# Attention and a squared-ReLU feed-forward on one core: the seven half-size products in another order, their joins on GpSimd, and queued work spread out

## The chip, the cores and the metric

The kernel runs on one core of a Trainium2 chip. A core has five engines that work through queues of their own: TensorE (PE; its weight loads are listed apart as PEld), VectorE (DVE), ScalarE (ACT), GpSimd (POOL) and SyncE (SP), which here issues the DMAs. They wait for each other by semaphores. SBUF is the on-chip memory of 128 partitions, PSUM the eight banks into which TensorE writes. The metric is the device time of one execution in microseconds (us). Every number is float32, and one float32 matmul of the program appears in the trace as two records ("passes").

## The reference

Eight batches of twelve heads, 448 rows, head dimension 64. Rows of q and k are normalized, softmax attention follows, the heads are put side by side (3584 tokens x 768), and a feed-forward layer with squared ReLU ends it:

```python
q_n, k_n = (rmsnorm(q, g_q), rmsnorm(k, g_k))
attn = softmax(q_n @ k_n.T / sqrt(64))      # per batch and head
x = (attn @ v).transpose(0, 2, 1, 3).reshape(3584, 768)
h = np.maximum(x @ w_in, 0.0)               # w_in 768 x 2048
out = (h * h) @ w_out                       # w_out 2048 x 768
```

w_in and w_out arrive as 64-bit numbers and are turned into float32 on the chip ("words").

## The kernel before, in words

**Feed-forward.** It runs in four passes u = 0 to 3, each over two batches (896 rows), and each pass in NBLK = 4 blocks of hidden columns. A block has a first product (x by w_in), the activation, and a second product (hidden by w_out, added into nine accumulators, `accs`). Both products are done with seven half-size products instead of eight (Strassen-Winograd, `PRODUCTS`: for instance P5 = S1 x T1), for which sums of operands are made beforehand: of w_in (S1 to S4), of w_out (T1 to T4), of x (`form_steps`) and of the hidden values (`hidden_sum`, L1037, on GpSimd: s1 = a21 + a22, s2 = s1 - a11, s4 = a12 - s2, s3 = a11 - a21).

In pass 0, `first_products` (L870) does the first product at this one level, while the weights are still converted (`convert`: load of words, three ScalarE instructions L1198 to L1200, three VectorE instructions L1211, L1231, L1235), the sums made (`make_sum`, L1304) and the sums for a second level are written to DRAM (`deep_steps`, L1271 and L1272, pieces `in_deep`). In passes 1 to 3, `deep_products` does each of the seven products at the second level again (11 matmuls of 224 columns, L921, in steps `step(k, 0..3)`), with pieces loaded four products ahead (`load_piece`, L798). `DEEP` lists the seven in order, with the place of each result: four quarters of the hidden tiles "11", "12", "21", "22", or a room "R". `put` moves a result out of PSUM: a copy on ScalarE where there is no base, else an addition on VectorE (L908). Where "R" holds a partial sum, more L908 additions join it to "12", "22" and "21". `activate` does Relu and Square on ScalarE (L977, L978); the last half of "21" is done by one VectorE instruction (L1014).

`second_products` (L1095) then runs, for each of three row tiles tt, the products in `SECOND_ORDER`, with `multiply_rest` (L1050) for the remaining 128 rows; `add_to` (L1138, VectorE) adds PSUM to the accumulator, or copies on ScalarE in block 0 (L1136). Three PSUM banks (`roles`) rotate; bank 1 also serves as `aside` in the deep products, banks 0 to 4 belong to attention.

**Attention.** It runs over 48 pairs of heads. The first batches are done before the feed-forward starts; afterwards a visit to a pair (`visit_among`, `visit_whole`) is put between steps of the feed-forward: scores (L405), exponentials on ScalarE (`weigh`, L413), values (L490), denominators (L533, L542), sums of weights on GpSimd (`add_up`, L432). `place(u, x)` says at which cost a visit comes. `ffn(u)` is a generator whose steps yield a cost (`COST_IN`, `COST_OUT`, `COST_DEEP`); `run(until)` takes steps until that cost is spent, and after each step lets queued work go: one weight sum, the end of a conversion, conversions that are due (`late`), up to two steps of the next pass's forms (`follow_plan(2)`), and one or two each of `tasks` and `pool_tasks` (`run_tasks`). A visit first runs all that is left of both queues. The instructions of each engine run in the order in which this program issues them.

**Transfers.** All loads and stores go through SyncE's queue in order: q and k rows (L157, L166), v (L348, L355), q rows to DRAM and back in blocks (`store_q` L314 and L320, `load_blocks` L330), words (L1179, L1184), half-size weights (L798), w_out's forms (L803), results (L1143). A DMA that waits for its source or its room holds back those behind it.

## Time and profile before

| | |
|---|---|
| median of 6 runs | 1460.32 us (1456.67 to 1463.01) |
| the profiled execution | 1462.95 us |
| its span, first to last instruction | 1460.8 us |
| mean granted TensorE clock | 0.988 |
| DMAs | 229.04 MB, q1 53.7% of 16 engines |

A group of the profile reads: line, engine, operation, out<-in by names, shapes, count | busy time, mean ns of one | idle time of the engine before them and what ended it. "bank L533 <- ACT wT L413: 14.4, 3, 5.5" in the list of waits means that TensorE's matmuls of line 533 waited for the ScalarE instruction of line 413 for 14.4 us in all, three times, at most 5.5. A row of busy time by stage gives a stretch, its length, busy time and number of instructions per engine, the granted clock (1.00 is full speed) and DMA.

### The profile page before, as it was taken

The numbers are of one execution on the slowest core, as the hardware profiler recorded it, in microseconds if no ns is written. First come the engines' busy times: TensorE is split into PE (matmuls) and PEld (weight loads), VectorE is DVE, ScalarE is ACT, GpSimd is POOL, SyncE is SP. The second block draws the span as 40 slices with busy tenths as digits, with TensorE's granted clock in tenths as the row PEclk, the third lists the DMA queues.
The fourth block names the chain that finished last, engine by engine and source line by source line (L and its number), as shares of the span: only waits on it lengthen the run. The fifth ranks groups of instructions, "written<-read, shape, count | busy, mean of one in ns | idle before, by whom it ended". The sixth has DMA issues, their size and how long they took to land.

```text
span 1460.8 us, 18011 instructions
## 1 busy us (share of the span) xinstructions
PE 1397.4 (96%) x5772; PEld 840.7 (58%) x5772; DVE 849.6 (58%) x1727; ACT 563.7 (39%) x1078; POOL 745.9 (51%) x750
## 2 busy tenths in 40 slices
PE   7989999899898989999999989999999999999998
PEld 3333444344443466665857548575676658678694
DVE  5996566687677754355544755345464665254554
ACT  6874466445555233341432323433332302221120
POOL 5667764656556865365473863736463462020201
PEclk9999999999999999999999999999999999999999
DMA  5555746767748874562747547265554426233232
GB/s 143 148 159 154 194 123 160 217 169 201 233 113 262 241 211 140 142 179 73 228 106 230 138 138 222 69 190 137 173 136 144 145 72 234 95 118 144 69 141 78
DMA packets 362219, 229.04 MB, mean 157 GB/s; under 512 B 270084, under 2 KB 339588, under 8 KB 358020
## 3 DMA queue, kind: packets, MB, share of 16 engines
q1 hardware_dynamic: 361824, 227.74, 53.7%
q8 instruction: 47, 0.77, 0.2%
q14 instruction: 56, 0.46, 0.1%
q10 hardware_dynamic: 292, 0.07, 0.0%
HBM read 172.49 MB, written 55.25 MB: 156 GB/s over the span
## 4 chain that ended last, share of the span: by engine, by line
PE 79%; DVE 6%; DMA 4%; issue 3%; POOL 3%; SPq 2%; ACT 2%; DVEq 0%; POOLq 0%; ACTq 0%
PE bank L1095 28%; PE bank L921 21%; PE bank L405 8%; PE bank L490 8%; PE bank L870 6%; PE bank L1050 5%; DVE hid L908 2%; DMA words<-in_moe_w_out_dram 1%; DMA in_sb<-in_deep 1%; PE bank L516 1%; SPq L157 1%; PE bank L533 1%; PE bank L502 1%; ACT wT L413 1%; POOL sum L432 1%
## 5 line engine op out<-in xcount | busy, mean ns | idle before, releaser
L921 PE MATMUL bank<-xT,in_sb 128*128 128x224 f32 x1344 | 294.7, 358 | 10.2 <-DMA in_sb<-in_deep 5.4
L1138 DVE TENSOR_TENSOR acc<-acc,bank 128x384 f32<-128x384 f32 x324 | 173.2, 549 | 215.5 <-PE bank L1095 188.8
L1095 PE MATMUL bank<-out_sb,hid 128*128 128x384 f32 x768 | 268.8, 487 | 3.8 <-DVE acc L1138 3.8
L921 PEld LDWEIGHTS bank<-xT,in_sb 128*128 128x128 f32 x1344 | 255.5, 192 | 24.4 <-issue 8.7
L1095 PE MATMUL bank<-out_sb,sums 128*128 128x384 f32 x576 | 204.5, 490 | 5.2 <-DVE acc L1138 5.2
L1095 PEld LDWEIGHTS bank<-out_sb,hid 128*128 128x128 f32 x768 | 145.2, 190 | 108.7 <-DVE acc L1138 6.6
L413 ACT ACTIVATE wT<-bank,rr 128x448 f32<-128x448 f32 x288 | 161.5, 630 | 114.3 <-PE bank L405 95.0
L202 POOL TENSOR_TENSOR rr<-ms,minus_half 128x8 f32<-128x8 f32 (+1 forms) x96 | 146.9, 1530 | 63.1 <-DVE ms L195 57.5
L1037 POOL TENSOR_TENSOR sums<-hid 128x384 f32<-128x384 f32 x32 | 32.9, 1028 | 274.8 <-ACT hid L978 238.1
L405 PE MATMUL bank<-qT,kT 64*128 64x448 f32 (+1 forms) x768 | 166.6, 576 | 2.1 <-DVE qT L378 1.1
L1095 PEld LDWEIGHTS bank<-out_sb,sums 128*128 128x128 f32 x576 | 107.4, 190 | 90.9 <-DVE acc L1138 10.7
L870 PE MATMUL bank<-xT,in_sb 128*128 128x448 f32 x336 | 137.1, 563 | 0.0
L908 DVE TENSOR_TENSOR part<-part,bank 128x224 f32<-128x224 f32 (+1 forms) x180 | 69.7, 415 | 97.8 <-PE bank L921 92.0
L405 PEld LDWEIGHTS bank<-qT,kT 64*128 64x128 f32 (+1 forms) x768 | 57.6, 174 | 99.6 <-issue 67.4
L432 POOL TENSOR_TENSOR sum<-sum,wT 128x448 f32<-128x448 f32 (+1 forms) x96 | 113.4, 1199 | 0.8
L870 PEld LDWEIGHTS bank<-xT,in_sb 128*128 128x128 f32 x336 | 64.6, 197 | 72.6 <-issue 65.0
L490 PE MATMUL bank<-wT,vt 128*64 128x448 f32 x480 | 102.8, 549 | 0.0
L977 ACT ACTIVATE hid<-hid 128x448 f32<-128x448 f32 x84 | 48.4, 576 | 130.2 <-DVE hid L908 130.2
L1050 PE MATMUL bank<-out_sb,hid 128*128 128x384 f32 x256 | 90.4, 491 | 0.0
L554 POOL COPY few<-few 32x14 f32<-32x14 f32 x48 | 9.0, 188 | 155.1 <-DVE few L552 153.1
L908 DVE TENSOR_TENSOR hid<-hid,bank 128x224 f32<-128x224 f32 (+1 forms) x180 | 66.6, 397 | 31.0 <-PE bank L921 28.6
L921 PE MATMUL bank<-more,in_sb 128*128 128x224 f32 x288 | 75.1, 362 | 6.9 <-DVE part L908 6.0
(131 smaller groups left out, 1871.2 us busy)
## 6 DMA issues: line engine op xcount, KB each, us to landing
in_sb<-in_deep SPq DMA_DIRECT2D x84, 640.0 KB, 4.2
out_sb<-out_forms SPq DMA_DIRECT2D x24, 1536.0 KB, 8.6
words<-in_moe_w_in_dram SPq DMA_DIRECT2D x32, 384.0 KB, 3.7
words<-in_moe_w_out_dram SPq DMA_DIRECT2D x32, 384.0 KB, 3.4
out_forms<-out_sb SPq DMA_DIRECT2D x8, 1536.0 KB, 6.4
qk<-in_q_dram SPq DMA_DIRECT2D x96, 96.0 KB, 3.0
qk<-in_k_dram SPq DMA_DIRECT2D x96, 96.0 KB, 2.6
vt<-in_v_dram SPq DMA_DIRECT2D x96, 96.0 KB, 3.1
```

The costliest lines, as they stand in the source:

```text
L202: self.nc.gpsimd.tensor_tensor(out=self.rr[i][:, x, 0 : self.count(i)], in0=ms, in1=self.minus_half.to_broadcast(list(ms.shape)), op=ALU.pow,)
L405: nc.tensor.matmul(sc[some], lhsT=turned[p, 1][r, keys], rhs=turned[p, 0][r, :], start=True, stop=True,)
L413: nc.scalar.activation(new_weights((i, m), e), sc, AF.Exp, scale=rows.rr[i][:, 1, 2 * m + e : 2 * m + e + 1],)
L432: nc.gpsimd.tensor_tensor(out=sums[i, e][some], in0=left[some], in1=weights[key_of(i, m), e][some], op=ALU.add)
L490: nc.tensor.matmul(values_bank(i)[ds(e * D, D), :], lhsT=lasts[i % 2][mine, e, :] if m == NJ else values[i][:, m, e, :], rhs=weights[key_o ...
L870: nc.tensor.matmul(ps, lhsT=w_sb[:, IN.index(left), c, :], rhs=forms[u, c][right], start=first and c == 0, stop=c == NK - 1, skip_group_ch ...
L908: nc.vector.tensor_tensor(out=dst, in0=left, in1=right, op=ALU.add)
L921: nc.tensor.matmul(ps, lhsT=left, rhs=right, start=start, stop=stop, skip_group_check=True)
L977: nc.scalar.activation(dst, dst, AF.Relu)
L1050: nc.tensor.matmul(ps, lhsT=hid[a].rearrange("p t e s -> p t (e s)")[:, t, ds(NT * P, P)], rhs=w_sb[t][:, 2 * a + half, :], start=(a, t) = ...
L1095: nc.tensor.matmul(ps, lhsT=lefts[left][:, t, ts(tt, P)], rhs=w_sb[t][:, OUT.index(right), :], start=first and t == 0, stop=t == 1, skip_g ...
L1138: nc.vector.tensor_tensor(out=acc, in0=acc, in1=ps, op=ALU.add)
```

## The change

- `DEEP`: the seven products come in the order 11x11, S4x22, S2xT2, 12x21, S1xT1, S3xT3, 22xT4. Results go straight to "11", "12", "21", "22"; only S3xT3 goes to a room ("part"). Three products, instead of two, have no base and leave PSUM by ScalarE copies.
- Six additions per block (`join`, 128x448 each) on GpSimd take the place of the VectorE joins; the VectorE activation (L1014) becomes Relu and Square on ScalarE.
- The second product is given to `deep_products` as the generator `second`: P1 of tt = 0 is issued before the last two matmuls of the seventh product; then the order is `FIRST_OF_BLOCK`, with the rest in banks 2 and 1. All eight hidden sums are issued after P1. During this, `held` keeps back `pool_tasks` (from the fifth product's third step) and `tasks` (from the seventh's first step); a visit empties both all the same.
- In passes 1 to 3 transfers of q, k and v go to a queue `transfers`, from which one or two are issued per step (`slowly`). The forms' plan takes one step instead of two, sees a pair of heads four steps later (`arrive`), and its pauses end the turn.
- The stores of the deep sums are issued one step after the sum; the deep sums wait until the weight sums are done and are completed in the middle of the next block instead of its end. Conversions of w_in are due earlier in a block.
- The visits' places in passes 1 to 3 move to 99, 321 and 451 of a block's 481 cost units (the last to the end of the pass).

```diff
...
     def room_for_blocks(i, x):
         return rows.room(i)[:, x].rearrange("p g h d -> p (g h d)")[:, ds(i % 2 * S, S)]
 
+    def transfer(to, some):
+
+        if slowly:
+            transfers.append((to, some))
+        else:
+            nc.sync.dma_start(to, some)
+
+    def follow_transfers(most):
+        for _ in range(min(len(transfers), most)):
+            nc.sync.dma_start(*transfers.popleft())
...
         if u - 1 not in through_with and (b % 2 * NPAIR + c) < 8:
             away[b, c] = dram.tile([P, S], F32, name="x_rows", tag="x_rows", bufs=8)
             nc.sync.dma_start(away[b, c], xts.pop((b, c)))
-        here.add((b, c))
+        arriving.append([4, (b, c)])
+
+    def arrive(all_=False):
+
+        for some in arriving:
+            some[0] -= 1
...
             if tiles > free.get(max(through_with), 0) or not here.issuperset(x):
                 break
             plan.popleft()
-            step()
-            most -= 1
+            if step is not None:
+                step()
+            most = most - 1 if step else 0
...
     }
 
     FIRST_ORDER = ["P1", "P5", "P2", "P6", "P3", "P4", "P7"]
+    FIRST_OF_BLOCK = ["P1", "rest0", "P5", "P4", "P6", "P2", "rest1", "P3", "P7"]
     SECOND_ORDER = ["P1", "P2", "P5", "P6", "P4", "P3", "P7"]
     COST_IN, COST_OUT, COST_DEEP = 12 * NK // 2, 10, 3
...
 
 
     DEEP = [
-        ("P1", "11", "11", "R", None), ("P5", "S1", "T1", "22", None),
-        ("P2", "12", "21", "11", "R"), ("P6", "S2", "T2", "R", "R"),
-        ("P3", "S4", "22", "12", "22"), ("P7", "S3", "T3", "R", "R"),
-        ("P4", "22", "T4", "21", "R"),
+        ("11", "11", "11", None), ("S4", "22", "12", None), ("S2", "T2", "21", "11"),
+        ("12", "21", "11", "11"), ("S1", "T1", "22", "21"), ("S3", "T3", "part", None),
+        ("22", "T4", "21", "21"),
     ]
...
                 load_piece(((u - 1) * NBLK + blk) * 7 + k + 4)
                 if blk == NBLK - 1:
                     let_go(u, right)
+            for some in then.get((k, n), ()):
+                some()
+
+        def join(name, t, other="part"):
+            dst = to[name][:, t]
+            nc.gpsimd.tensor_tensor(out=dst, in0=dst, in1=to[other][:, t], op=ALU.add)
 
         def activate(name, t):
             dst = to[name][:, t]
             nc.scalar.activation(dst, dst, AF.Relu)
             nc.scalar.activation(dst, dst, AF.Square)
 
+        then = {
+            (3, 3): [lambda: activate("11", 0), lambda: activate("11", 1)],
+            (4, 2): [lambda: join("12", 0, "22")], (4, 3): [lambda: join("12", 1, "22")],
+            (5, 2): [lambda: join("22", 0), lambda: activate("12", 0)],
+            (5, 3): [lambda: join("22", 1), lambda: activate("12", 1)],
+            (6, 2): [lambda: activate("22", 0), lambda: activate("22", 1)],
+            (6, 3): [lambda: join("21", 0), lambda: join("21", 1)],
+        }
         for k in range(8):
-            if k < 7:
-                step(k, 0)
-            if k:
-                step(k - 1, 2)
-            yield (3 * (k < 7) + 3 * (k > 0)) * COST_DEEP
-            if k == 7:
-                activate("21", 0)
-                multiply_rest(u, blk, hid, roles[1:3], ((0, 0), (0, 1)), halves=(0,))
-                yield COST_OUT
-            else:
-                step(k, 1)
-            if k:
-                step(k - 1, 3)
-            if k == 3:
-                for t in range(2):
-                    activate("11", t)
-            elif k == 4:
-                add(to["12"][:, 0], to["12"][:, 0], to["R"][:, 0])
-                add(quarter("12", 3), quarter("12", 3), quarter("R", 3))
-            elif k == 5:
-                add(quarter("12", 2), quarter("12", 2), quarter("R", 2))
-                for t in range(2):
-                    activate("12", t)
-            elif k == 6:
-                for t in range(2):
-                    add(to["22"][:, t], to["22"][:, t], to["R"][:, t])
-                    activate("22", t)
-                add(quarter("21", 3), quarter("21", 3), quarter("R", 3))
-                for n in range(2):
-                    for t in range(2):
-                        hidden_sum(hid, sums_, t, n)
-            elif k == 7:
-                last = to["21"][:, 1]
-                nc.vector.scalar_tensor_tensor(
-                    out=last, in0=last, scalar=0.0, in1=last, op0=ALU.max, op1=ALU.mult
-                )
-                multiply_rest(u, blk, hid, roles[1:3], ((0, 0), (0, 1)), halves=(1,))
-            yield (3 * (k < 7) + 2 * (k > 0)) * COST_DEEP + (k == 7) * COST_OUT
+            for p, n in ((k, 0), (k - 1, 2), (k, 1), (k - 1, 3)):
+                if (p, n) == (4, 2):
+                    held.add("pool")
+                elif (p, n) == (6, 0):
+                    held.add("others")
+                elif (p, n) == (6, 3):
+                    yield next(second)
+                if 0 <= p < 7:
+                    step(p, n)
+                    yield (2 if n == 3 else 3) * COST_DEEP
+        for t in range(2):
+            activate("21", t)
 
     def hidden(dst, left, right, op):
         nc.vector.tensor_tensor(out=dst, in0=left, in1=right, op=op)
...
         ns = out_of(u, blk)
         w_sb = [out_sb[n] for n in ns]
         s1, s2, s4 = sums_
-        for n, t in [(n, 1) for n in range(4)] if not u else [(3, 0), (3, 1), (2, 0), (2, 1)]:
-            hidden_sum(hid, sums_, t, n)
+
+        def make_sums(*some):
+            for n in some:
+                for t in (0, 1) if u else (1,):
+                    hidden_sum(hid, sums_, t, n)
 
         if u:
-            turn_roles(0, 2, 1)
+            turn_roles(1, 2, 0)
         else:
+            make_sums(0, 1, 2, 3)
             for some in (PARTS[:3], PARTS[3:]):
                 multiply_rest(u, blk, hid, roles, some, accs[-1] if (1, 1) in some else None)
...
             upper_acc, lower_acc = accs[2 * tt], accs[2 * tt + 1]
             c11, c12 = [upper_acc[:, ts(h, HALF)] for h in range(2)]
             c21, c22 = [lower_acc[:, ts(h, HALF)] for h in range(2)]
-            for name in SECOND_ORDER:
+            order = SECOND_ORDER if tt or not u else FIRST_OF_BLOCK
+            engine = nc.scalar if order is SECOND_ORDER else nc.vector
+            for name in order:
+                if name.startswith("rest"):
+                    a = int(name[-1])
+                    multiply_rest(
+                        u, blk, hid, banks[2:0:-1], PARTS_BY_ROW[2 * a : 2 * a + 2],
+                        accs[-1] if a else None,
+                    )
+                    if a:
+                        held.discard("others")
+                    yield 2 * COST_OUT
+                    continue
                 role, first, left, right = PRODUCTS[name]
                 ps = roles[role][:, 0:HALF]
                 for t in range(2):
...
                         skip_group_check=not first,
                     )
                 if name == "P1":
-                    add_to(c11, ps, blk == 0)
-                    if u and tt == 0:
-                        multiply_rest(u, blk, hid, roles[2:0:-1], ((1, 0), (1, 1)), accs[-1])
+                    add_to(c11, ps, blk == 0, engine)
+                    if order is FIRST_OF_BLOCK:
+                        make_sums(0, 1)
+                        yield COST_OUT
+                        make_sums(2, 3)
...
             made[n] = ffn_p.tile([P, 4, P], F32, name="more", tag="more", bufs=4)[:, 0:size]
             left, right = [x() for x in (left, right)]
             next(sum_engines).tensor_tensor(out=made[n], in0=left, in1=right, op=op)
-            nc.sync.dma_start(keep[:, some, n], made[n])
-
-        steps = [raw]
+            to_keep.append((keep[:, some, n], made[n]))
...
                 steps.append(
                     lambda s=some, n=n, le=left, ri=right, op=op: derive(s, n, le, ri, op)
                 )
-        return steps
+
+        def both(make):
+            if len(to_keep) > 1 or not make:
+                nc.sync.dma_start(*to_keep.popleft())
+            if make:
+                make()
...
     ahead = 4 * tile_pieces
     early = deque(2 + 2.4 * n for n in range(ahead + 1))
     every = block / ahead
-    late = deque(
-        block + 2 + every * (n - 2 * tile_pieces) for n in range(len(all_pieces) - ahead)
-    )
+    late = deque()
+    for n in range(len(all_pieces) - ahead):
+        blk, m = divmod(n, ahead)
+        late.append(blk * block + 2 + ((0.42 + 0.05 * m) * block if m < ahead // 2 else (
+            block + every * (m - ahead // 2)
+        )))
 
     load_weights(0)
...
 
     VISITS, last = 2, len(pairs) - 1
     unit = 2 * NPAIR * VISITS
-    tasks, pool_tasks = deque(), deque()
+    tasks, pool_tasks, held = deque(), deque(), set()
 
     def place(u, x):
 
         if u == 0:
             return COST * x / unit
         block = LATER // NBLK
-        end = block - COST_SECOND - 2 * COST_DEEP
-        at = [0, end]
-        for b in range(NBLK - 1):
-            at += [b * block + end + block // 3, (b + 1) * block + 84, (b + 1) * block + end]
-        at += [LATER - COST_SECOND // 2, LATER]
+        second = block - COST_SECOND
+        offsets = (second * 3 // 7, second + 9 * COST_OUT, second + 22 * COST_OUT)
+        at = [0] + [b * block + some for b in range(NBLK) for some in offsets]
+        at[-1] = LATER
...
-        nonlocal spent
+        nonlocal spent, slowly
+        slowly = not first
         while spent < until:
             cost = next(stream)
             spent += cost
+            if deep_to_make and not sums_to_make:
+                deep_to_make.popleft()()
             make_sum()
             end_join()
-            if first and deep_to_make:
-                deep_to_make.popleft()()
             while first and late and late[0] <= spent:
                 late.popleft()
                 convert()
-            follow_plan(2)
+            arrive()
+            follow_plan(1)
             run_tasks(2 if cost > COST_OUT else 1)
 
     def run_tasks(most):
-        for some in (tasks, pool_tasks):
-            for _ in range(min(len(some), most)):
+        for name, some in (("others", tasks), ("pool", pool_tasks)):
+            for _ in range(0 if name in held else min(len(some), most)):
                 some.popleft()()
+        follow_transfers(most)
+
+    def run_all():
+        before = set(held)
+        held.clear()
+        while tasks or pool_tasks:
+            run_tasks(len(tasks) + len(pool_tasks))
+        held.update(before)
...
```

## The prediction

> **What bounds the kernel now.** I read the first section of the page, then the busy time by stage, then who waited for whom on TensorE, then the instruction groups of VectorE and GpSimd by shape. All times are microseconds unless marked ns.
>
> ```profile
> PE 1397.4 (96%) x5772; PEld 840.7 (58%) x5772; DVE 849.6 (58%) x1727; ACT 563.7 (39%) x1078; POOL 745.9 (51%) x750
> ```
>
> TensorE is busy for 1397.4 of 1460.8. The change keeps all matmuls, so 63.4 of idle time, and whatever the clock gate costs inside the busy time, is all that can be won. By stage (columns: stretch, its length, busy time of PE, PEld, DVE, ACT, POOL, granted clock, DMA share, GB/s; one row per block of the four passes u = 0 to 3):
>
> ```profile
> 0.00:135.00 135.00, 121.92 (x704) 46.89 (x708) 106.77 (x241) 91.38 (x173) 83.79 (x79) 0.99 0.60 156
> ...
> 230.00:328.00 98.00, 90.83 (x289) 41.05 (x289) 73.48 (x125) 50.34 (x99) 58.33 (x48) 0.97 0.66 186
> 328.00:425.00 97.00, 90.93 (x292) 41.55 (x288) 70.61 (x125) 51.86 (x102) 58.28 (x49) 0.98 0.70 196
> 425.00:525.00 100.00, 92.95 (x309) 42.64 (x308) 73.01 (x122) 42.38 (x81) 72.71 (x67) 0.98 0.73 218
> 525.00:608.00 83.00, 80.94 (x339) 55.17 (x336) 32.78 (x77) 33.17 (x65) 45.49 (x48) 0.96 0.54 149
> ...
> 773.00:877.00 104.00, 94.42 (x409) 57.86 (x409) 61.35 (x123) 33.70 (x63) 64.93 (x76) 1.00 0.59 178
> 877.00:955.00 78.00, 74.94 (x319) 51.62 (x319) 32.88 (x76) 29.34 (x57) 42.82 (x45) 0.98 0.50 136
> ...
> 1120.00:1206.00 86.00, 81.73 (x350) 54.15 (x349) 51.25 (x98) 19.65 (x37) 42.89 (x56) 0.98 0.41 140
> ...
> 1331.00:1393.00 62.00, 61.78 (x255) 47.90 (x255) 31.57 (x71) 10.30 (x20) 8.12 (x8) 1.00 0.36 126
> ```
>
> The last row is a block of the last pass, where no attention runs beside it: 0.2 idle in 62. The block end that the change rebuilds is therefore already tight when nothing disturbs it. The idle time lies in the disturbed blocks: 20.8 in the first pass (135 to 525), 13.3 in the second, 9.0 in the third. A clock below 1.00 is more loss: (1 - clock) x length gives 2.9 + 1.9 + 2.0 in the first pass, 3.3, 1.6 and 1.7 in the rows at 525, 877 and 1120. What those waits are (total, times, longest):
>
> ```profile
> PE bank L533 <- ACT wT L413: 14.4, 3, 5.5
> PE bank L1095 <- DVE acc L1138: 9.0, 9, 3.3
> PE bank L921 <- DVE part L908: 6.0, 4, 2.0
> PE bank L921 <- DVE hid L908: 5.5, 9, 1.5
> PE bank L921 <- DMA in_sb<-in_deep: 5.4, 3, 3.1
> ```
>
> and, behind the first of them, ScalarE's own wait, which keeps the exponentials (L413) in its queue:
>
> ```profile
> ACT words L1198 <- DMA words<-in_moe_w_out_dram: 29.3, 5, 10.1
> ```
>
> **The change, part by part.** The built program's order shows the same matmuls and the same DMAs; VectorE has 120 instructions fewer, ScalarE 48 more, GpSimd 72 more (six joins in each of 12 blocks).
>
> *Joins move from VectorE to GpSimd.* The rows:
>
> ```profile
> L908 DVE TENSOR_TENSOR hid<-hid,part 128x448 f32<-128x448 f32 x36 | 21.4, 622 | 0.0
> L908 DVE TENSOR_TENSOR hid<-hid,part 128x224 f32<-128x224 f32 x36 | 17.7, 491 | 0.4
> L1014 DVE SCALAR_TENSOR_TENSOR hid<-hid 128x448 f32<-128x448 f32 x12 | 10.8, 903 | 0.4
> ...
> L432 POOL TENSOR_TENSOR sum<-sum,wT 128x448 f32<-128x448 f32 x48 | 56.2, 1186 | 0.2
> ```
>
> (These come from the two engines' own lists.) VectorE sheds 21.4 + 17.7 + 10.8 = 49.9, GpSimd gains 72 x 1.19 = 86. Both have room on average: GpSimd is at 43 to 48 of some 83 in a loaded block and gets 7 more. What counts is the place: the stops behind L908 sit where joins stand between evictions in VectorE's queue. They are 6.0 + 5.5 plus the 1.7 of clock in the row at 1120; 4 x 0.2 belong to the undisturbed last pass and stay. At most 12.4 can go, at least 0 if VectorE is late with other work; I take **-10**, near the upper end, because the join leaves the queue altogether.
>
> The Trainium skill, "GPSIMD Engine Reference", section Engine selection, sends a two-input add to VectorE since GpSimd takes about twice as long. The rows agree on the ratio (1186 against 622 ns). Followed strictly, with joins on the path, the sum would be 86 - 39 = 47 slower; by the rows VectorE's time here is on TensorE's path and GpSimd's mostly is not.
>
> *Block end.* New order of the products: 11; S4x22; S2xT2; 12x21; S1xT1; S3xT3; 22xT4, the last partial results joined on GpSimd, and the second product's P1, the rest (rows 384 to 447 and 0 to 63) and P5, P4, P6 put around the last two products. Count from when TensorE leaves the last matmul of S3xT3 (time 0). TensorE: 1.1 (six passes of 0.19), P1 1.3 (four passes of 0.32), last two matmuls 0.75, rest 2.6, so P5 at 5.8, P4 7.1, P6 8.4, P2 9.7, second rest 11.0 and, after another 2.6, P3 13.5, P7 14.8. The other queues: copy 0.35 and latency, join of "22" until 1.8; Relu and Square of two halves (0.58 each, "12" before "22") until 4.0; then L1037's sums at 1.03 to 1.09 each: s1 5.1, s2 7.2; joins of "21" 9.6; its activation 10.7; s4 11.8; s3 14.0. P5 has 0.7 to spare, P6 1.2, P2 waits about 0.5 (its first half can start), P7 0.8 to spare. Now the block loses 0.2 to 0.5 at this place. So **0** in the four undisturbed blocks. In the eight loaded ones GpSimd still carries the weight sums and normalization of the visit before (six adds of 1.2, two multiplies of 1.25, eight small copies of 0.19: 11 in a stretch of 6 of TensorE time), and each microsecond by which it is late beyond 0.7 arrives at P5 or P2. Bounds: 0, and 14 GpSimd instructions all at 1.5 (the slowest single L432) instead of 1.15, 4.9 x 8 = 39. I take 0.5 x 8 = **+4**, as half of the visits leave about 1 of backlog and GpSimd tasks are held back from the product before. Queued behind the join of "21" are s4, s3 and then the pow of the next pair, which nobody needs for a visit; behind ScalarE's activation of "12" is one eviction of S3xT3, which the three rotating banks cover.
>
> *Rest in banks 1 and 2.* The rest now ends in banks 2 and 1 and a visit's scores follow at once into banks 0, 1, 2, 3. TensorE must wait for the add of bank 1 (0.55 by L1138, plus 0.2 of latency): 0.75 x 8 = **+6**. Bounds 0 (if another matmul comes between) and 1.5 x 8 = 12 (a full pair of scores later). Tasks held during the block end are flushed at that same visit, VectorE and ScalarE having some 3 more to do before the exponentials: **+2**, bounds 0 and 8, since the attend matmuls (2.4) cover it.
>
> *First pass.* Conversions of "in" weights move from 0.50..0.94 of a block to 0.42..0.77, the deep sums follow at once, each store is issued a step after its sum, so SyncE no longer stands waiting for the sum with a words load behind it. ScalarE's waits for words (29.3) are where L533's 14.4 come from; with the 6.8 of clock in these three blocks 21.2 can go. I take **-12**, more than half: the store of q rows and its reload still stand in SyncE's queue. The cost is density: from half to the end of such a block VectorE has 41 to 43 busy in 52, and some 3.4 of deep sums (5 of 0.68) come in. Bounds 0 and 3 x 5; I take 1 per block, **+3**.
>
> *Queued transfers.* Loads of q, k, v go out one or two per step, so the loads of half-size weights (in_sb) come ahead of them. Of the 5.4 waited and at most 4.9 of clock (rows 525 and 877) I take **-5**: the reload of q rows still blocks the queue for its round trip. L1095's 9.0 come from bursts of form subtractions; one step at a time instead of two, and four steps later, takes **-2** (bounds -9 and +3).
>
> The Trainium skill, "TensorE: Matmul & The Clock Gate", section What's actually happening, halves the clock only after an idle window of about 3.4. Here a stop of 2.06 before 545.46 is already followed by some 3.5 of double spacing between matmuls. By the rule the 2 us stops would be worth only their length and the sum some 3 smaller; the measurement decides.
>
> ScalarE's 48 more instructions (0.35 to 0.58, about 22 in all) cost 0: it is busy 28 to 33 of 83 in these blocks; without that cover they would stand before exponentials, 2 per block.
>
> **Sum.** -10 + 0 + 4 + 6 + 2 - 12 + 3 - 5 - 2 = -14. The profiled execution took 1462.95 (2.15 around its span), 2.6 above the median; 1462.95 - 14 = 1448.9, so against the median 1460.3 - 14 = **1446.3**.
>
> **Rivals.**
> 1. *GpSimd becomes the bound of the block end* (the slower side). If its chain is late by 4 instead of 0.5 in loaded blocks, 8 x 3.5 = 28 more: 1474. It decides against the change from 8 x 2.3, that is 2.3 per loaded block. For: the whole chain of joins and sums now lies between the last product and P5, P2, P3, and single GpSimd adds run up to 1.5. Against: no two-input VectorE work stands there now, and the queue is held free. 0.20.
> 2. *The words still come late.* The -12 fails, the rest stands: 1458. For: the reload of q rows blocks SyncE for 4 at a time, and this is not changed in the first pass. Against: the stores of deep sums stood between. 0.15.
> 3. *VectorE saturates in the first pass*: +12 over my +3, 1458 or, with rival 2, 1470. For: 82% busy already. Against: three banks rotate. 0.07.
> 4. *All waits go* (-21.2 - 12.4 - 10.3 - 9 + 10 to 15 = -38 to -43): 1420. For: each has a mechanism in the change. 0.13.
>
> **How the numbers follow.** The forecast has 0.45, its own range 1436 to 1456. The range for 8 in 10 runs from 1424 (most of rival 4 left out below) to 1474 (rival 1 taken in, its worse half left out). 0.2%, about 2.9, is what a measurement of this kernel can tell from no change. Faster: the forecast, rival 4, and nearly half of 2 and 3, 0.66. Same: the rest of rivals 2 and 3, 0.09. Slower: rival 1, and the worse part of 2 and 3, 0.25.
>
> **What would show it.** Right: the row of L533 waits falls below 6; the stops behind L908 fall below 3; GpSimd's busy time rises by 80 to 90 while VectorE's falls by about 50; blocks of the last pass stay at 62. Wrong: new rows of L1095 (its successor line) waiting for sums or "hid" from GpSimd or ScalarE above 10 in total; score matmuls waiting for the rest's add above 8; first-pass waits for VectorE above 10.

## The result and the profile after

The changed kernel takes 1456.03 us (median of 19 runs, 1447.42 to 1463.54) where the kernel before takes 1461.23 beside it. The ratio is 0.9962 (95% interval 0.9951 to 0.9973): 5.6 us faster, where 14.0 were forecast. The profiled execution took 1457.0 us, its span is 1455.1. The first part of the page after:

```profile
PE 1395.7 (96%) x5772; PEld 839.5 (58%) x5772; DVE 790.4 (54%) x1607; ACT 582.9 (40%) x1126; POOL 818.1 (56%) x822
```

GpSimd has 72.2 more and VectorE 59.2 less than before; TensorE has the same 5772 records. What it waits for (total, times, longest), whole execution:

```profile
PE bank L417 <- ACT qT L353: 9.2, 4, 3.7
PE bank L944 <- DMA in_sb<-in_deep: 6.3, 3, 2.6
PE bank L1114 <- DVE acc L1167: 6.2, 4, 2.8
PE bank L382 <- POOL qk L217: 5.2, 4, 3.0
PE bank L502 <- DMA lasts<-in_v_dram: 3.9, 1, 3.9
...
PE bank L545 <- ACT wT L425: 3.2, 2, 2.6
...
PE bank L944 <- ACT part L941: 3.0, 4, 1.0
PE bank L944 <- ACT wT L425: 2.9, 4, 0.8
...
PE bank L944 <- ACT hid L941: 0.8, 2, 0.4
...
PE bank L944 <- DVE hid L929: 0.4, 2, 0.2
```

L545 is the old L533, L929 the old L908, L944 the old L921, L1114 the old L1095. The rows that the prediction aimed at have shrunk: 14.4 became 3.2, 11.5 became 0.4. In their place stand scores that wait for a transposed qT (9.2, where the kernel before had 0.9), and two stops ahead of the feed-forward (5.2 and 3.9, where it had 2.1 and 2.3). Part of the 11.5 has only changed its engine: the deep products now wait 3.0 + 0.8 for ScalarE's copies out of PSUM (L941; before 0.3, for L953) and 2.9 for its exponentials, a row that the kernel before did not have. Busy time by stage (the columns as before):

```profile
0.00:135.00 135.00, 116.90 (x660) 44.33 (x660) 104.28 (x233) 88.28 (x168) 82.84 (x79) 0.95 0.68 179
...
230.00:328.00 98.00, 91.06 (x292) 41.18 (x291) 68.78 (x120) 54.50 (x105) 56.68 (x48) 0.97 0.68 189
328.00:425.00 97.00, 89.46 (x282) 40.80 (x281) 69.54 (x121) 51.88 (x101) 55.30 (x47) 0.96 0.69 192
425.00:525.00 100.00, 97.33 (x324) 45.71 (x324) 69.15 (x121) 41.00 (x78) 65.44 (x58) 1.00 0.71 209
...
773.00:877.00 104.00, 101.88 (x444) 64.16 (x443) 58.44 (x120) 36.50 (x70) 71.94 (x84) 1.00 0.59 182
...
1331.00:1393.00 62.00, 62.00 (x258) 48.30 (x257) 27.49 (x61) 12.38 (x25) 14.54 (x14) 1.00 0.36 128
```

The windows are those of before, though the work in them has moved by up to 16 us. The first row is a stage that the prediction never priced: TensorE busy for 116.9 of 135 where it was 121.9, and a clock of 0.95 where it was 0.99. The row at 773 shows the opposite, 2.1 idle in 104 where there were 9.6.

Block ends are better for an account by stage (the start of the last second-product record of each block, read from the trace; differences are taken before rounding):

| stage | before | after | difference |
|---|---|---|---|
| up to the first product of the feed-forward | 135.9 | 143.5 | +7.6 |
| pass 0, four blocks | 381.2 | 380.6 | -0.7 |
| pass 1 | 349.9 | 342.4 | -7.5 |
| pass 2 | 338.2 | 335.1 | -3.1 |
| pass 3 | 248.8 | 246.9 | -2.0 |

So the later passes won 12.6. The first pass won next to nothing, though its wait for the exponentials that stand behind the words is nearly gone, and the stretch ahead of it lost 7.6.

### The profile page after: what moved, and what is told of

Read it like the earlier page. It is cut to its first block, busy times and chain, and to the rows that moved or that the text cites. A ratio compares the mean times of both kernels' runs of the same rounds, so it can differ in the third digit from the quotient of the medians.

```text
span 1455.1 us, 18023 instructions
## 1 busy us (share of the span) xinstructions
PE 1395.7 (96%) x5772; PEld 839.5 (58%) x5772; DVE 790.4 (54%) x1607; ACT 582.9 (40%) x1126; POOL 818.1 (56%) x822
## 4 chain that ended last, share of the span: by engine, by line
PE 77%; DMA 5%; DVE 5%; POOL 4%; ACT 3%; issue 3%; SPq 2%; POOLq 0%; DVEq 0%; ACTq 0%
PE bank L1114 27%; PE bank L944 21%; PE bank L417 8%; PE bank L502 7%; PE bank L1053 5%; PE bank L890 5%; DMA words<-in_moe_w_out_dram 2%; DMA in_deep<-more 1%; SPq L315 1%; DMA in_sb<-in_deep 1%; PE bank L528 1%; POOL xT L662 1%; PE bank L554 1%; PE bank L514 1%; POOL sum L444 1%
## 5 line engine op out<-in xcount | busy, mean ns | idle before, releaser
L944 PE MATMUL bank<-xT,in_sb 128*128 128x224 f32 x1344 | 292.4, 356 | 9.4 <-DMA in_sb<-in_deep 6.3
L1114 PE MATMUL bank<-out_sb,hid 128*128 128x384 f32 x768 | 272.2, 491 | 5.2 <-DVE acc L1167 2.7
L944 PEld LDWEIGHTS bank<-xT,in_sb 128*128 128x128 f32 x1344 | 254.8, 192 | 22.5 <-ACT wT L425 8.6
L1114 PE MATMUL bank<-out_sb,sums 128*128 128x384 f32 x576 | 207.0, 492 | 3.5 <-DVE acc L1167 3.5
L1114 PEld LDWEIGHTS bank<-out_sb,hid 128*128 128x128 f32 x768 | 144.1, 191 | 112.6 <-ACT hid L998 7.9
L417 PE MATMUL bank<-qT,kT 64*128 64x448 f32 (+1 forms) x768 | 169.7, 576 | 10.6 <-ACT qT L353 9.2
L929 DVE TENSOR_TENSOR hid<-hid,bank 128x224 f32<-128x224 f32 x312 | 111.5, 384 | 114.9 <-PE bank L944 101.9
L1114 PEld LDWEIGHTS bank<-out_sb,sums 128*128 128x128 f32 x576 | 108.4, 191 | 87.5 <-DVE acc L1167 7.5
L890 PE MATMUL bank<-xT,in_sb 128*128 128x448 f32 x336 | 131.6, 545 | 0.0
L993 POOL TENSOR_TENSOR hid<-hid 128x448 f32<-128x448 f32 x24 | 27.2, 1140 | 170.7 <-DVE hid L929 150.4
L417 PEld LDWEIGHTS bank<-qT,kT 64*128 64x128 f32 (+1 forms) x768 | 57.8, 174 | 113.4 <-issue 74.4
L502 PE MATMUL bank<-wT,vt 128*64 128x448 f32 x480 | 103.1, 549 | 0.4 <-DMA vt<-in_v_dram 0.4
L997 ACT ACTIVATE hid<-hid 128x448 f32<-128x448 f32 x96 | 54.9, 572 | 119.7 <-POOL hid L993 62.6
L890 PEld LDWEIGHTS bank<-xT,in_sb 128*128 128x128 f32 x336 | 62.2, 190 | 68.6 <-issue 61.6
L944 PE MATMUL bank<-more,in_sb 128*128 128x224 f32 x288 | 75.3, 356 | 3.0 <-ACT part L941 3.0
L179 ACT ACTIVATE squares<-qk 128x512 f32<-128x512 f32 (+1 forms) x68 | 39.5, 581 | 89.4 <-DVE ms L192 45.2
```

The lines of the kernel that those rows point to most:

```text
L417: nc.tensor.matmul(sc[some], lhsT=turned[p, 1][r, keys], rhs=turned[p, 0][r, :], start=True, stop=True,)
L502: nc.tensor.matmul(values_bank(i)[ds(e * D, D), :], lhsT=lasts[i % 2][mine, e, :] if m == NJ else values[i][:, m, e, :], rhs=weights[key_o ...
L890: nc.tensor.matmul(ps, lhsT=w_sb[:, IN.index(left), c, :], rhs=forms[u, c][right], start=first and c == 0, stop=c == NK - 1, skip_group_ch ...
L929: nc.vector.tensor_tensor(out=quarter(name, n), in0=quarter(base, n), in1=ps, op=ALU.add)
L944: nc.tensor.matmul(ps, lhsT=left, rhs=right, start=start, stop=stop, skip_group_check=True)
L997: nc.scalar.activation(dst, dst, AF.Relu)
```

## The experiments

Ratios are against the kernel before, on the same chip. In us I put them on a kernel before of 1461.2, so 0.001 is 1.46.

My theory after the result was that the later passes gain 12.6 by themselves, and that the edits to conversions and deep sums (due times, late stores, sums made in `begin`) cost about as much as they save. The rival was that the head's loss belongs to this one execution, and that VectorE is simply full in the first pass.

**1. No deep sums ahead of the feed-forward.**

```diff
     def begin(step):
-        if deep_to_make and not sums_to_make:
-            deep_to_make.popleft()()
```

> Deep sums are no longer made in the stretch before the feed-forward (no pop in `begin`); all else is the changed kernel (1456.0, first product at 143.5 us, head clock 0.95). Theory A (the deep sums made there hold GpSimd and SyncE's queue, and cost the head its 7.6): the first product starts at 136 to 138, TensorE's stops behind GpSimd's L217 and behind `lasts` fall to what they were before (5.2 to 2, 3.9 to 0), and the time falls by 5 to 7.6, to 1448 to 1451. Theory B (the head was slow for another reason, a load that came late or the clock of that execution): the start stays at 141 or later and the time at 1456 +- 2. Theory C (the work is only put off): the start comes at 136 and the first block grows by as much, since its VectorE has the sums to make: 1454 to 1457.

Measured: 1453.21 us, ratio 0.9935 (0.9919 to 0.9951), 4 us better than the changed kernel, the intervals just touching. Theory A holds for the head: the first product starts at 135.7, though the stop behind `lasts` falls only to 2.7, about what it was before. Theory C is right as well: the first block grows from 89.7 to 96.6, and the profiled execution, 2.8 above the median and with a span of 1454.2, is only 0.9 shorter. Two windows of the head, 10 and 8 us long, first the changed kernel:

```profile
87.00:97.00 10.00, 6.08 (x19) 1.95 (x17) 5.43 (x11) 3.60 (x7) 2.98 (x4) 0.66 0.86 210
112.00:120.00 8.00, 5.67 (x18) 2.81 (x20) 7.47 (x15) 3.44 (x7) 5.75 (x5) 0.59 0.93 247
```

and without the pops:

```profile
87.00:97.00 10.00, 10.00 (x62) 3.60 (x60) 9.46 (x22) 6.99 (x13) 3.92 (x4) 1.00 0.52 140
112.00:120.00 8.00, 8.00 (x54) 2.84 (x50) 5.83 (x16) 5.18 (x10) 5.56 (x4) 1.00 0.80 201
```

With the pops, DMA is at 0.86 and 0.93 instead of 0.52 and 0.80, TensorE stands at 87 for `lasts`, whose load SyncE issues at 88.8 instead of 84.7, behind five stores of the deep sums' pieces (L1290 and L1292, 5.9 together), and at 111 for the normalization. GpSimd does that, and here waits until 111.8 for VectorE's row sums (L195). The clock falls to 0.66 and 0.59 (columns 8 and 9 are clock and DMA). The head's loss is the pops', not chance: in the three kernels that have them the first product starts at 143.5 to 143.7, in all the others of these experiments at 133.6 to 138.5.

**2. Stores of deep sums at once.**

```diff
-            to_keep.append((keep[:, some, n], made[n]))
+            nc.sync.dma_start(keep[:, some, n], made[n])
```

(`both` and `to_keep` go with it.)

> Each store of a deep sum is issued at once after its sum again, not a step later; all else is the changed kernel. Theory A (the store that comes a step later gives the four `more` buffers back late, so VectorE and GpSimd stand in order before the deep sum, and qT behind them): VectorE's wait for `in_deep<-more` falls from 25.2 to below 16, GpSimd's from 24.8 to below 12, TensorE's stops behind qT from 9.2 to below 4, and the time by 4 to 8, to 1448 to 1452; ScalarE's wait for words may rise again from 34 by some. Theory B (qT stands behind the conversions themselves, since VectorE is full): stops behind qT stay above 6, the words come later, and the time is 1456 to 1460.

Measured: 1454.66, ratio 0.9947 (0.9928 to 0.9967). This can't be told from the changed kernel. In the profiled execution, 6.9 above the median, VectorE's wait for `in_deep<-more` fell from 25.2 to 18.7, but TensorE's stops behind qT only from 9.2 to 6.8. Neither theory's time was met: the late stores hold the buffers, as A says, but most of what keeps qT waiting is something else.

**3. All edits to conversions and deep sums undone.** Experiments 1 and 2, and in addition the uniform `late` of before, the pop after `make_sum` in the first pass only, and `make_all_deep` at the block's end.

> All edits to the conversions and the deep sums are undone (due times, stores, pops, where a block completes them); block end, DEEP, held queues, transfers, plan and visits stay changed. Theory A (the changes of the first pass and the head cost as much as they bring, the gain of 12.6 in the three later passes is independent of them): head near 136, first pass 381 to 384, later passes 924.4, so 1461.2 - 12.6 = 1448.6, with the wait of TensorE for wT in the first pass back at 14 and words at 58. Theory B (the later passes gain only because the first pass left its sums in time, or the first pass is better by what was taken from it): the first pass becomes longer than before's 381.2 by 5 or more, or the later passes lose: 1454 to 1460.

Measured: 1450.90, ratio 0.9918 (0.9902 to 0.9935), clear of the changed kernel's interval. Theory A, within a microsecond: 1449.2 for the 1448.6 expected. The head ends at 135.9, the first pass takes 382.0, and this kernel's wait for wT is that of before:

```profile
PE bank L545 <- ACT wT L425: 14.9, 4, 5.5
```

So the first-pass edits as a whole cost 6.4 us, though they took 11.7 off this row. The following experiments start from this kernel, called E4 here (e4_first_pass_before in the expectations).

**4. Only the due times put back**, on E4 (`late` of the changed kernel).

> The kernel e4_first_pass_before (ratio 0.9918, words waits 60 us, TensorE behind wT in the first pass 15.5 us) with only the earlier due times of the conversions (0.42 to 0.77 of a block) put back; stores at once, no pops before the feed-forward, sums as before. Theory A (the due times are the part that takes the words waits off, the stores and pops are the part that cost): words waits below 40, TensorE behind wT below 6, first pass 8 to 12 shorter, ratio 0.984 to 0.988. Theory B (earlier conversions only crowd VectorE, and the stops move to qT and the accumulators): stops behind wT fall but others rise by as much, ratio 0.990 to 0.994.

Measured: 1448.15, ratio 0.9887 (0.9866 to 0.9908): 4.5 us faster than E4 (the intervals overlap a little), between A and B. The waits of this kernel:

```profile
PE bank L943 <- DMA in_sb<-in_deep: 9.6, 4, 3.4
PE bank L417 <- ACT qT L353: 8.8, 4, 4.5
PE bank L545 <- ACT wT L425: 5.1, 2, 3.2
```

wT falls from 14.9 to 5.1, and qT rises from 0.9 to 8.8: the transposition that VectorE does for qT now stands behind the conversions that came forward. The largest such stop of the changed kernel shows it (start, length, then the idle time before it and what ended it; L1240, L1260 and L1264 are the conversions on VectorE, L1227 to L1229 those on ScalarE, L351 and L353 transpose and scale qT):

```profile
383.21 0.55 DVE L1260 SCALAR_TENSOR_TENSOR in_sb<-words,in_sb 128x384 uint32<-128x384 uint32 x1
...
383.90 0.56 DVE L1264 CUSTOM_DVE_ANT_0 in_sb<-words,in_sb 128x768 uint16<-128x768 uint16 x1
...
384.38 0.35 DVE L1240 TENSOR_SCALAR in_sb<-words 128x384 uint32<-128x384 uint32 x1
384.65 0.64 DVE L351 STREAM_TRANSPOSE qT<-qk 128x448 f32<-128x448 f32 x1
...
384.78 0.56 ACT L1227 ACTIVATE words<-words 128x384 f32<-128x384 f32 x1 [0.19 <-DMA words<-in_moe_w_in_dram]
...
385.24 0.54 ACT L1228 ACTIVATE words<-words 128x384 f32<-128x384 uint32 x1
...
385.81 0.55 ACT L1229 ACTIVATE words<-words 128x384 uint32<-128x384 f32 x1
...
386.26 0.65 ACT L353 ACTIVATE qT<-qT,g 128x448 f32<-128x448 f32 x1
...
386.96 1.76 PE L417 MATMUL bank<-qT,kT 64*64 64x448 f32 x4 [3.72 <-ACT qT L353]
```

The scaling on ScalarE stands behind conversions too: the transposition ends at 385.3, the scaling starts at 386.3. So TensorE got back 9.8 in one row and lost 7.9 in the other.

From this kernel to the changed one it is 11.0 (0.9887 to 0.9962): what the pops, the late stores and the new place where the deep sums are completed cost together. The pops are 4 of it by experiment 1, the stores 2 by experiment 2, within its noise; the rest was not measured by itself.

**5. Joins on VectorE**, on the changed kernel.

```diff
-            nc.gpsimd.tensor_tensor(out=dst, in0=dst, in1=to[other][:, t], op=ALU.add)
+            nc.vector.tensor_tensor(out=dst, in0=dst, in1=to[other][:, t], op=ALU.add)
```

> The six joins of a block are done by VectorE (0.62 each) and not by GpSimd (1.14 each), at the same places of the program; all else is the changed kernel. Theory A (the joins between evictions were what TensorE waited for): VectorE 790 to about 835 busy, GpSimd 818 to about 736; TensorE's stops behind L929 come back from 0.4 to 6 or more, later passes 6 to 12 longer, 1462 to 1468. Theory B (the stops went with the new order and the held queues, not with the engine): stops behind L929 stay below 2 and, since a join is 0.5 shorter on the chain to P5 and P2, the time is 1453 to 1457.

Measured: 1460.72, ratio 0.9986 (0.9972 to 1.0000), 3.5 us slower than the changed kernel, the intervals just touching. VectorE 845.1, GpSimd 749.2. Both theories missed: the stops behind L929 are 0.2, as B says, yet the time rose. Undisturbed blocks of the last pass take 62.0 again instead of 61.6, which gives 1.4 over the pass; what the rest is, the waits do not show.

**6. No queue of transfers**, on E4 (`slowly = False` throughout).

> e4_first_pass_before without the queue of transfers: loads of q, k, v and the trips of q rows go to SyncE at once, as before the change. Theory A (my term of -5: the queue lets loads of half-size weights come first): TensorE's stops behind in_sb<-in_deep rise from 7.5 in the later passes to 12 or more and the ratio from 0.9918 to 0.995 or more. Theory B (those stops have the same size with and without the queue, as before and after suggest with 5.4 and 6.8): stops stay at 5 to 8, ratio 0.991 to 0.993. Theory C (spreading them makes them late): stops fall below 4, ratio below 0.990.

Measured: 1455.62, ratio 0.9949 (0.9934 to 0.9964), 4.5 slower than E4, the intervals just touching. Stops behind in_sb rose from 7.0 to 9.9, less than A asked, but the time agrees with A and with the term of -5. In the profiled execution 1.9 of the 3.4 by which it is longer lie after the last block's end, so the way there is not settled.

**7. The visits' places of before**, on E4.

```diff
-        second = block - COST_SECOND
-        offsets = (second * 3 // 7, second + 9 * COST_OUT, second + 22 * COST_OUT)
-        at = [0] + [b * block + some for b in range(NBLK) for some in offsets]
-        at[-1] = LATER
+        end = block - COST_SECOND - 2 * COST_DEEP
+        at = [0, end]
+        for b in range(NBLK - 1):
+            at += [b * block + end + block // 3, (b + 1) * block + 84, (b + 1) * block + end]
+        at += [LATER - COST_SECOND // 2, LATER]
```

> e4_first_pass_before with the visits' places of the kernel before (382, 84 and a third of a block on). Theory A (the places bring much of the 12 that the later passes won, since a visit no longer falls on the end of the first product): passes 1 and 2, 342.8 and 337.0, grow to 349 and 339, ratio 0.996 or more. Theory B (the block end and the joins bring it, wherever the visits lie): 343 and 337, ratio 0.991 to 0.993. If the visit now falls on the seventh product and empties what is held, GpSimd's chain is late there: stops of L1113 behind ACT hid and of P2 behind the sums above 8.

Measured: 1443.52, ratio 0.9866 (0.9847 to 0.9885), 7.6 us *faster* than E4. No theory of mine had that sign. Passes 1 and 2 take 339.2 and 328.9 instead of 342.7 and 337.0. The stops of L943 behind VectorE's evictions rise from 0.3 to 5.4, and still it wins. The score matmuls from 517 to 1206 us, by shape (E4 first, then this kernel; the last number is idle time before them):

```profile
L417 PE MATMUL bank<-qT,kT 64*128 64x448 f32 x276 | 69.6, 571 | 0.0
```

```profile
L417 PE MATMUL bank<-qT,kT 64*128 64x448 f32 x276 | 64.9, 571 | 0.0
```

The same 276 records take 4.7 more in E4, with no idle time in front: the wait lies between the records, at their weight loads. The changed kernel's timeline of weight loads at one such place (start, length, then the idle time before it and what ended it):

```profile
670.48 0.29 PEld L417 LDWEIGHTS bank<-qT,kT 64*128 64x128 f32 x2 [0.55 <-issue]
671.20 0.33 PEld L417 LDWEIGHTS bank<-qT,kT 64*128 64x128 f32 x4 [0.42 <-DVE acc L1167]
```

The scores follow the rest, and those for bank 1 wait for VectorE's add of that bank. This accounts for 4.7 of the 7.6; the remainder was not traced.

**8. That visit one product later**, on E4: P3 is issued between the rest and the scores.

```diff
-        offsets = (second * 3 // 7, second + 9 * COST_OUT, second + 22 * COST_OUT)
+        offsets = (second * 3 // 7, second + 10 * COST_OUT, second + 22 * COST_OUT)
```

> e4_first_pass_before with one of the three visits of a block one product later: P3 stands between the second rest and the scores. In e4 the first eight records of the scores after the rest (L1052) take 2.34 to 2.42 us until the next line and 1.70 elsewhere, seven times. Theory A (this is the wait for the adds of the rest's banks, my term of +6): they take 1.70, score matmuls fall from 80.5 to about 75.5 and the ratio from 0.9918 to 0.988 to 0.990. Theory B (the adds are late for another reason, VectorE being behind at that place): the wait moves to P7 or the values, and the ratio stays at 0.991 to 0.993.

Measured: 1446.12, ratio 0.9873 (0.9847 to 0.9899), 6.6 faster than E4 and clear of its interval. Theory A: all groups of eight records take 1.70, and the row of the same 276 records reads

```profile
L417 PE MATMUL bank<-qT,kT 64*128 64x448 f32 x276 | 64.6, 571 | 0.0
```

One product between the rest and the scores gives back 6.6 of the 7.6 that the new places cost, 5.0 of it in this row.

**9. Plan of before**, on E4 (`follow_plan(2)`, heads seen at once, pauses that count as steps), and **10. the new plan alone**, on the kernel before.

> e4_first_pass_before with the next pass's sums of x as before: two steps of the plan a turn, no four turns of delay, pauses that count as steps. Theory A (bursts of these subtractions in VectorE's queue were the whole of the accumulators' stops, 6.8 in the later passes before and none after): stops of L1113 behind DVE acc come back to 5 or more in the later passes, ratio 0.9918 to 0.996 to 0.997. Theory B (my term of -2: most of those stops came from L908 joins and adds at the block end in VectorE's queue, not from the plan): stops below 3, ratio 0.991 to 0.9935.

> The kernel before with the plan alone changed: one step a turn, heads seen four turns later, pauses that end a turn. Theory A (bursts of form subtractions in VectorE's queue cost the kernel before most of what the later passes won): TensorE's stops behind DVE acc fall from 6.8 to below 2 and those behind L908 from 12.6 to below 7 in the later passes; ratio 0.990 to 0.994. Theory B (my term of -2; the +14 of e11_plan_before came because the changed kernel has twice as many turns in a block, so that two steps a turn were a denser plan than the one of before): ratio 0.9975 to 1.000.

Measured: on E4 1465.78, ratio 1.0016 (1.0004 to 1.0029), 14.3 slower. On the kernel before 1451.68, ratio 0.9932 (0.9919 to 0.9945), 9.9 faster. The larger number has a part that the change itself made: `deep_products` now yields about twice as often, so two steps a turn are a denser plan than they were. The 9.9 is free of that. One stretch of the second pass, first the kernel before, then the same with the new plan:

```profile
773.00:868.00 95.00, 85.72 (x370) 53.82 (x371) 56.36 (x110) 27.55 (x51) 57.23 (x67) 1.00 0.58 169
```

```profile
773.00:868.00 95.00, 92.15 (x411) 58.05 (x410) 58.76 (x123) 33.70 (x63) 60.38 (x69) 1.00 0.66 196
```

and the rows that moved with it, in the second kernel (L1104 is L1095 of before, L917 its L908):

```profile
PE bank L930 <- DVE part L917: 6.3, 5, 2.3
PE bank L930 <- DVE hid L917: 4.4, 9, 1.0
PE bank L1104 <- DVE acc L1147: 3.2, 4, 1.3
```

The accumulators' wait falls from 9.0 to 3.2, and the 3.2 are the first pass's. The stops behind evictions are 10.7 instead of 11.5: theory A's half about L908 fails, its ratio holds. TensorE gets 6.4 more done in 95 us (the second kernel's block ends at 858.7, so its row holds some of the next), which is also more than the wait row names.

**11. Nothing held back at the block end**, on E4 (`held` stays empty).

> e4_first_pass_before with nothing held back at the block end (`held` stays empty, so weight sums, normalization and tasks go on between the last products and the sums). Theory A (rival 1 of the prediction was only kept off by the holding: GpSimd's chain would be late at P5 and P2 in loaded blocks): TensorE's stops at L1113 behind ACT hid or GpSimd's sums rise from 2.3 to 8 or more, ratio from 0.9918 to 0.995 or more. Theory B (the chain has room or the queues are empty there anyway): stops below 4, ratio 0.990 to 0.9935.

Measured: 1462.83, ratio 0.9997 (0.9984 to 1.0011), 11.5 slower than E4. Theory A. Its rows, from a profiled execution 6.7 above the median:

```profile
PE bank L1113 <- ACT hid L997: 6.8, 13, 2.0
...
PE bank L1113 <- POOL sums L1038: 2.9, 6, 1.2
```

In E4 the first of these is 1.6 and the second is absent; ScalarE's own wait for GpSimd's joins rises from 62.6 to 73.3. The mechanism of the first rival, GpSimd's chain late at the block end, is real, and the holding keeps it off. `held` also keeps back tasks of other engines; their share of the 11.5 was not measured by itself.

**12. The block end alone**: plan, transfers and places of before on E4.

> The new block end alone (order and destinations, joins on GpSimd, second product interleaved, held queues): first pass, visits' places, plan and transfers as before. By the separate steps measured so far (places -7.6, transfers +4.5, plan +14 from 1450.9 of e4): 1462, ratio 0.9995 (0.997 to 1.002). Theory A (the block end gains nothing by itself, since the plan of two steps a turn is now twice as dense in its finer turns): this number. Theory B (the terms are not additive: with the old places a visit does not fall on the block end and the plan costs less there): ratio 0.988 to 0.995.

Measured: 1456.46, ratio 0.9962 (0.9947 to 0.9976): 5.6 us faster, between the theories. With the plan of two steps in its finer turns, the accumulators' wait is 7.6 and the evictions' 8.9, yet it wins. The ratio is by chance that of the whole change. From here to the kernel of experiment 7 plan and transfers bring 14.0, where on E4 they bring 14.3 + 4.5: the steps depend on each other. That the plan of two steps costs less where no visit falls among the rests would explain it, but is not shown.

**13. What gained by itself, together**: the changed kernel with the `begin` of before, stores at once, sums as before and the visits' old places; the due times stay.

> Of the changed kernel what gained by itself: block end, plan, transfers, earlier due times; stores, pops and visits' places of the kernel before. If the gains add (0.9866 of e10_places_before, less 0.0031 of the due times): ratio 0.9835 (0.981 to 0.986), about 1437. Rival: in_sb stops, which rose to 10.2 with the due times, take it back: 0.986 to 0.988.

Measured: 1436.81 (1433.58 to 1438.44), ratio 0.9827 (0.9811 to 0.9843). It beats both kernels, by 25 and by 20 us, and the gains added within 1.2. Its first page line and its waits:

```profile
PE 1382.8 (96%) x5772; PEld 835.4 (58%) x5772; DVE 797.2 (56%) x1607; ACT 580.7 (40%) x1126; POOL 822.2 (57%) x822
```

```profile
PE bank L417 <- ACT qT L353: 8.7, 4, 4.5
PE bank L943 <- DVE hid L928: 5.5, 5, 1.5
PE bank L943 <- DMA in_sb<-in_deep: 4.8, 2, 3.4
```

TensorE is busy for 12.9 less than in the changed kernel with the same matmuls: the mean granted clock is 0.995 against 0.987, and the score matmuls (64*128) take 137.0 instead of 142.0.

**14. The joins on VectorE in that kernel.**

> e13_best (ratio 0.9827, stops of L943 behind DVE L928 6.9) with the six joins on VectorE. Theory A (with the visits at their old places, where evictions stop TensorE, the engine of the joins matters as the prediction had it, -10): stops behind L928 rise to 12 or more and the ratio to 0.988 or more. Theory B (the joins' engine is worth the 3.5 of e6_join_dve and the rest of those stops comes from the tasks of a visit): stops at 8 to 11, ratio 0.984 to 0.987.

Measured: 1443.19, ratio 0.9863 (0.9838 to 0.9888), 5.3 slower than experiment 13, the intervals just meeting. Theory B by its time; the waits' row rises less than it said:

```profile
PE bank L943 <- DVE hid L928: 6.9, 10, 1.4
```

So the joins' engine is worth 3.5 to 5.3, with the visits here or there. The rest of the stops behind VectorE's evictions (11.5 before, 8.9 in experiment 12, 5.4 in experiment 7, 0.3 in E4) went with the new order, the plan and, above all, the visits' new places.

## Why the prediction was right and wrong

The sign was right, the size was not: 5.6 instead of 14.0.

- **The step that failed is the first pass's, -12 with +3 for density.** It measured +6.4 (experiment 3). Its mechanism was half right. The waits for wT fell to 3.2, below the 6 named as the sign, and the due times alone bring 4.5. Two things were missed. Conversions that come forward stand in the queues of VectorE and ScalarE before the transposition and scaling of qT, for which TensorE now waits 9.2 where it waited about 1; I had asked only which engine is full, not who stands behind the moved work. And I did not follow the deep sums out of `run` into `begin`: made ahead of the feed-forward they cost the head 7.6, by their stores ahead of a load of v and by a later normalization; the first block gives 6.9 of this back. Some 5 of the 11 that the edits other than the due times cost are not assigned to any of them.
- **The plan's -2 was far too small.** Alone it is -9.9, about the bound of -9. The cause was named rightly, bursts of subtractions in VectorE's queue, but only 2 of the 9.0 were taken, without a reason. The wait row fell by 5.8, all that it had in the later passes, and the time by more; the row at 773 of before, 9.6 idle at full clock, was on the page.
- **Scores after the rest, +6:** right. Seven groups took 0.64 to 0.72 longer than 1.70 in E4, 4.8 in all; moving the visit gave 6.6. That wait is not under a row of L417 behind DVE acc: a reader who looks for it there, as the prediction's last part told him to, finds nothing.
- **Evictions, -10:** the row went as forecast, 11.5 to 0.4, but 3.8 of new waits stand behind ScalarE's copies and 2.9 behind its exponentials. The cause is only in part the one given: the joins' engine brings 3.5 to 5.3, the rest is order, plan and places.
- **Block end 0, GpSimd +4:** undisturbed blocks went from 62.0 to 61.6, a small gain, not a loss. In loaded blocks L1114 waits 1.7 behind ScalarE's hid. Rival 1's mechanism comes as soon as nothing is held (+11.5 with all else that `held` keeps back, where the rival had 28). GpSimd's 72.2 and VectorE's -59.2 lie beside the forecast of 80 to 90 and -50.
- **Transfers, -5:** -4.5 by experiment 6, though the row of in_sb that was to carry it went from 5.4 to 6.3 in the change as a whole.
- **Task flush, +2,** was not measured by itself. Saturation of VectorE (rival 3) did not come as a wait for accumulators, 6.2 in the first pass where it was 3.2. With the 9.2 for qT beside it, though, the sign that the prediction gave for being wrong, first-pass waits for VectorE above 10, did come.

The terms beside the steps that were measured, each on another kernel and with some 2 to 3 us of noise:

| terms | forecast | measured | by |
|---|---|---|---|
| first pass, density | -12 + 3 = -9 | +6.4 | experiment 3 |
| plan | -2 | -9.9 | experiment 10 |
| evictions, block end | -10 + 0 + 4 = -6 | -5.6 | experiment 12 |
| transfers | -5 | -4.5 | experiment 6 |
| scores after the rest, flush | 6 + 2 = +8 | +7.6 | experiment 7 |
| sum | -14 | -6.0 | whole change: -5.6 |

So two errors of opposite sign, 15.4 too good for the first pass and 7.9 too poor for the plan, make up nearly all of the 8.4 between 14.0 and 5.6. That evictions and block end together come out right is in part luck: in experiment 12 the row that was to carry the -10 only falls from 11.5 to 8.9, and the last pass alone gains 1.6.

## What to carry to other kernels

When work is moved forward on an engine, list what stands behind its new place in that queue, for every function that pops the queue of work, and price the first of those as the next wait. A wait row names who was late, not why: before pricing "evictions late" or "accumulators late", look at what else that engine did just before, in the stage with the most idle time at full clock. Where matmuls write again into a bank that has just been emptied, put one other product between them, as experiment 8 did: the price of not doing so hides between the records and shows only as busy time of the same records.

## What was not expected of the hardware

A stop of TensorE is paid more than once. In the changed kernel's head, after stops of 3.9 and 3.0 us (the rows of L502 and L382 above), the windows that follow show

```profile
91.20:96.00 4.80, 4.75 (x14) 1.46 (x14) 3.54 (x7) 0.00 (x0) 0.00 (x0) 0.50 1.10 267
...
114.30:118.30 4.00, 3.97 (x14) 2.34 (x16) 3.74 (x8) 1.97 (x4) 3.52 (x3) 0.50 0.97 282
```

a granted clock of 0.50, and transposes spaced 213 ns instead of 109. In the trace the clock falls at 89.5 and 113.4, some 2.2 and 2.1 us into these stops, and is back 6.8 us later. This is busy time, so the idle column does not hold it: of the 20 us between the changed kernel and experiment 13, 12.9 are in TensorE's busy time, 5.0 of them in the score matmuls and the larger part where the clock is lower. The rule that the prediction weighed (the Trainium skill, "TensorE: Matmul & The Clock Gate", section What's actually happening) puts the loss of clock behind an idle window of about 3.4 us; in this trace a stop of 3.0 was enough, and in that of before a stop of 2.3 ahead of 109 us was followed by a clock of 0.66 over 5 us.
